# Decode attention over two caches: VectorE on whole key tiles, one normalization per side, another mapping of an output weight, and a projection split into three runs

## The chip, the cores and the metric

The kernel runs on one core of a Trainium2 chip. The engines of that core are TensorE (PE in the profile, its weight loads PEld), VectorE (DVE), ScalarE (ACT), GpSimd (POOL) and SyncE (SP), which issues most of the transfers; sixteen DMA engines carry them. The metric is the device time of one execution in microseconds (us), as the median of several runs. The profile is of one further execution, and its times are counted from the start of that execution's span.

## What is computed

Two independent attention layers, A and B, each decode one token. Both have 32 heads of 128 elements, an input row of 512, and a cache of 16384 positions for each head. A attends to all 16384 positions, B only to the last 4096. The two output rows of 512 stand side by side in the result. Everything is bf16.

```python
def _A_ref(x, k_cache, v_cache, wq, wo):
    B, Sq, D = x.shape
    Hq, Dh = 32, 128
    ...
    q = (lambda x, *d: x.transpose(*d))((x @ wq).reshape(B, Sq, Hq, Dh), 0, 2, 1, 3)
    ...
    scores = jnp.einsum("bhqd,bhkd->bhqk", q, k) * (Dh ** -0.5)
    p = _softmax(scores, axis=-1)
    o = jnp.einsum("bhqk,bhkd->bhqd", p, v)
    return (lambda x, *d: x.transpose(*d))(o, 0, 2, 1, 3).reshape(B, Sq, Hq * Dh) @ wo

# _B_ref: the same, with W = min(4096, max(256, Sk // 4)) and
    k = jnp.repeat(k_cache[:, :, Sk - W:, :], rep, axis=1)
    v = jnp.repeat(v_cache[:, :, Sk - W:, :], rep, axis=1)
```

All keys and values that are attended to are read once: 128 MB each of K and V for A, 32 MB each for B (in units of 2^20 bytes), and four weight matrices of 4 MB. The profile counts 352.32 million bytes read.

## The kernel before

**Tiles and steps.** The work runs in 20 steps (`steps`, `NT`), 16 of A and 4 of B; B's are steps 0, 7, 13 and 19. A step handles one key tile and one value tile of 128 partitions x 256 positions x 128 elements, 8.4 million bytes each. For A such a tile is two whole heads, with 64 partitions a head and 256 neighbouring positions a partition. For B it is two halves (`parts` is 2), each of four heads with 128 positions a partition, and each half is a transfer of its own (`b_window`).

**Buffers.** Key tiles live in a ring of two buffers (`kring`), value tiles in a single one (`vring`). At the start `wqt`, which holds both query weights, has the value buffer, and `scratch`, which holds the input rows `x_row` and B's spread input `xb`, has a key buffer. At the end the output weights and the last value halves take these buffers over (`wot`): `W` holds A's wo and the first half of B's last values, `Z` the second half and B's wo.

**Queries.** `spread_x` writes the input, turned into columns by `turn_x`, into a matrix with zeros elsewhere, so that one matmul leaves each partition the query of its own head. `project_q` makes the queries from it and ScalarE stores them in `s.q`.

**Scores on VectorE.** For each half of the tile `scores_prod` (L227) multiplies the keys in place by the query, and `scores_tree` folds the 128 elements to 64, 32, 16 and 8 by additions in place (L233), and to one by a reduction (L237) into `sc`.

**Softmax and the product with V.** A step does this for the tile of the step before (`un`): `unit_max` takes each partition's maximum (L244) and PE transposes it into one row; `max_all` takes the maximum of each head in that row (L262), copies it out to all partitions' places in `Mr` (L264, L266), and PE turns it back into a column (L268). `soft` makes the bias and the exponentials with their sums `cs` on ScalarE (L276, L282). `spread_p` writes the probabilities, masked by head, to `pm` (L297). `soft_sum` adds the sums of each head's partitions on PE (L315), `recip` takes the reciprocal on VectorE (L323), `pv` multiplies by the values on PE (L331), `evict` copies the result out, scaled by the reciprocal (L340), and `columns` picks each head's column and stores it in `s.O` (L348, L352). The last tile has a way of its own: `pv_columns` multiplies with the value half as the stationary operand (L358) and scales by the reciprocal as it stores (L362).

**Output.** `permute_o` reorders the 128 x 32 matrix of outputs by means of a shifted identity, `pick`, so that it fits the order of the rows in `wo_t`. Before, partition p holds the 32 neighbouring rows 32p to 32p + 31 of wo. `project_out_rows` (A) does 32 matmuls that add up one row (L383). `project_out_columns` (B) does 128 small matmuls that take wo as the stationary operand, piece by piece as wo arrives (L397), adds up the pieces (L403), turns the columns to rows (L407), and stores them (L409, L410).

**Order.** Within `tc.manual_schedule()` each engine runs its instructions in the order of the program text. SyncE issues the transfers in that order, too, and a transfer whose buffer is still in use holds up those after it. At the start the order is B's wq, the first half of B's first keys, A's wq, the second half, then the keys of step 1. The input rows come in three transfers each on ScalarE's queue. In step T the order is: the values of step T - 1 (`load_v`, L132 and L141), the keys of step T + 1 (`load_k`, L117 and L123), then on VectorE the first product, `max_all` of the tile before, the first tree, the reciprocal, the second product and tree, and `unit_max`. In step 19 A's wo and the first value half follow, and after the loop the second value half and B's wo in five pieces of 16, 8, 4, 3 and 1 rows a partition (L157).

## Time and profile before

| | |
|---|---|
| median of 3 runs | 825.79 us (825.49 to 826.01) |
| the profiled execution | 825.66 us |
| its span, first to last instruction | 823.9 us |
| mean granted TensorE clock in it | 0.592 |
| transferred | 352.62 MB, mean 428 GB/s |
| longest VectorE groups | additions L233 344.9 us in 160; products L227 277.8 us in 32 (A) and 69.4 us in 8 (B); reductions L237 48.8 us in 40 |
| product with V, L331 | 92.3 us in 1024 matmuls (A), 17.2 us in 192 (B) |

A page of the profile gives first the busy time of each engine with its share of the span and its number of instructions, and then the busy shares in tenths over 40 equal slices. The part on DMA queues names q1, the queue of the kernel's transfers, and others, among them q8 and q14, on which the engines fetch their instructions. The chain is followed back from the last instruction: at each step to what released it. In lists of instructions a line gives the start and the duration in us, the engine (SPq is SyncE's queue of DMA issues), the source line, the operation with output and input, how many instructions were merged, and in brackets how long the engine had been idle before and what ended that. In tables by windows the columns are the window, its length, the busy time of PE, PEld, VectorE, ScalarE and GpSimd, the granted TensorE clock, the busy share of the DMA engines and the rate in GB/s; a transfer packet is counted where it begins, so that single windows come out above 1.

### The profile page before, as it was taken

To read this page: it belongs to the slowest core of one execution; us is meant where nothing else is said; L and a number is where in the kernel's file an instruction comes from. 1 tells how busy PE (TensorE), PEld (TensorE's weight loads), DVE (VectorE), ACT (ScalarE), POOL (GpSimd) and SP (SyncE) were. 2 spreads that over 40 slices of the span, in tenths; PEclk is the share of its full clock that TensorE was granted. 3 is DMA by queue.
4 is the path that set the end of the run, shared out by engine and by line. 5 is a ranking of instruction groups with operands and counts; after the bars stand their busy time and mean duration, and the time that the engine had idled before them with its cause. 6 is when DMAs were issued, how large, how long until landed. Compare 5 with 4: busy or idle time off the path is not lost.

```text
span 823.9 us, 4724 instructions
## 1 busy us (share of the span) xinstructions
PE 202.7 (25%) x1985; PEld 100.7 (12%) x1985; DVE 763.9 (93%) x353; ACT 60.1 (7%) x168; POOL 0.7 (0%) x6
## 2 busy tenths in 40 slices
PE   2702212203030303130312213030303020303175
PEld 0201100101010101010101101010101010101035
DVE  2899999999999999999999999999999999999980
ACT  0101000001010000100000000010100000000010
POOL 0000000000000000000000000000000000000000
PEclk9865656565565555565555565565656565556585
DMA  9999999999999999999999999999999999999997
GB/s 384 434 433 433 453 420 443 430 436 440 423 446 420 424 439 443 412 453 420 443 417 449 414 452 410 450 417 428 438 449 424 436 433 430 443 414 445 418 429 296
DMA packets 8107, 352.62 MB, mean 428 GB/s; under 512 B 915, under 2 KB 1046, under 8 KB 1302
## 3 DMA queue, kind: packets, MB, share of 16 engines
q1 hardware_dynamic: 8072, 352.33, 99.2%
q8 instruction: 15, 0.25, 0.1%
q14 instruction: 6, 0.05, 0.0%
q10 hardware_dynamic: 14, 0.00, 0.0%
HBM read 352.32 MB, written 0.00 MB: 428 GB/s over the span
## 4 chain that ended last, share of the span: by engine, by line
DMA 82%; PE 15%; DVE 1%; SPq 0%; issue 0%; ACTq 0%; ACT 0%; DVEq 0%
DMA vt<-in_A_v_cache_dram 65%; DMA vt<-in_B_v_cache_dram 13%; PE oA L331 11%; DMA wot<-in_B_wo_dram 4%; PE oB L331 2%; PE qp L203 2%; DMA scratch<-in_A_x_dram 2%; DVE kt L227 1%; SPq L141 0%; ACTq L419 0%; SPq L157 0%; PE out_cols L397 0%; ACT qB L207 0%; PE out_rows L407 0%; DVE rows L409 0%
## 5 line engine op out<-in xcount | busy, mean ns | idle before, releaser
L233 DVE TENSOR_TENSOR kt<-kt 128x8192 bf16<-128x8192 bf16 (+3 forms) x160 | 344.9, 2156 | 4.8
L227 DVE TENSOR_TENSOR kt<-kt,qA 128x16384 bf16<-128x16384 bf16 x32 | 277.8, 8683 | 11.0 <-DMA kt<-in_A_k_cache_dram 10.9
L331 PE MATMUL oA<-vt,pm 128*8 128x512 bf16 x1024 | 92.3, 538 | 132.1 <-DMA vt<-in_A_v_cache_dram 132.1
L227 DVE TENSOR_TENSOR kt<-kt,qB 128x16384 bf16<-128x16384 bf16 x8 | 69.4, 8680 | 6.3 <-ACT qB L207 6.3
L249 PE MATMUL sm<-identf,m 128*1 128x128 f32 x24 | 8.1, 370 | 227.3 <-DVE m L244 227.3
L331 PEld LDWEIGHTS <-pm 128*8 128x8 bf16 (+1 forms) x1216 | 37.3, 111 | 216.7 <-issue 196.3
L268 PE MATMUL sm<-one_f,Mr 1*128 1x1 f32 x48 | 12.9, 347 | 176.7 <-DVE Mr L264 147.1
L237 DVE TENSOR_REDUCE sc<-kt 128x128 f32<-128x1024 bf16 x40 | 48.8, 1220 | 2.7
L276 ACT ACTIVATE bias<-sm 128x1 f32<-128x1 f32 (+1 forms) x20 | 3.4, 172 | 420.8 <-PE sm L268 420.8
L268 PEld LDWEIGHTS sm<-one_f,Mr 1*128 1x128 f32 x48 | 11.2, 298 | 183.6 <-DVE Mr L264 152.2
L249 PEld LDWEIGHTS sm<-identf,m 128*1 128x1 f32 x24 | 1.7, 79 | 229.3 <-issue 216.2
L340 ACT ACTIVATE o<-oA,r 128x512 f32<-128x512 f32 x16 | 11.0, 688 | 220.5 <-PE oA L331 220.5
L331 PE MATMUL oB<-vt,pm 128*16 128x512 bf16 x192 | 17.2, 494 | 20.3 <-DMA vt<-in_B_v_cache_dram 16.2
L348 PE MATMUL oc<-selA,o 128*128 128x2 f32 x128 | 16.9, 254 | 12.7 <-ACT o L340 12.7
L348 PEld LDWEIGHTS oc<-selA,o 128*128 128x128 f32 x128 | 15.5, 191 | 20.8 <-ACT o L340 20.8
L297 ACT ACTIVATE pm<-p,maskA 128x256 bf16<-128x256 bf16 x32 | 14.5, 500 | 0.5
L315 PE MATMUL sm<-cs,rowsA 128*128 128x1 f32 x32 | 9.4, 362 | 14.3 <-ACT p L282 14.3
L282 ACT ACTIVATE p<-sc,bias 128x256 bf16<-128x256 f32 (+1 forms) x24 | 11.3, 470 | 0.6
L203 PE MATMUL qp<-wqt,xbA 128*128 128x512 bf16 x32 | 8.8, 444 | 6.0 <-DVE kt L227 6.0
L315 PEld LDWEIGHTS sm<-cs,rowsA 128*128 128x128 f32 x32 | 8.0, 310 | 15.7 <-ACT p L282 15.7
L203 PE MATMUL qp<-wqt,scratch 128*128 128x512 bf16 x32 | 9.9, 486 | 0.0
L362 DVE TENSOR_TENSOR OB<-ocol,r 128x4 bf16<-128x4 f32 x2 | 0.3, 161 | 10.2 <-PE ocol L358 10.2
(71 smaller groups left out, 108.1 us busy)
## 6 DMA issues: line engine op xcount, KB each, us to landing
kt<-in_B_k_cache_dram SPq DMA_DIRECT2D x8, 4096.0 KB, 29.1
vt<-in_B_v_cache_dram SPq DMA_DIRECT2D x6, 4096.0 KB, 23.3
wot<-in_B_v_cache_dram SPq DMA_DIRECT2D x2, 4096.0 KB, 22.6
wqt<-in_B_wq_dram SPq DMA_DIRECT2D x1, 4096.0 KB, 12.3
wqt<-in_A_wq_dram SPq DMA_DIRECT2D x1, 4096.0 KB
wot<-in_A_wo_dram SPq DMA_DIRECT2D x1, 4096.0 KB
wot<-in_B_wo_dram SPq DMA_DIRECT2D x1, 2048.0 KB
wot<-in_B_wo_dram SPq DMA_DIRECT2D x1, 1024.0 KB
```

The source lines that it names most:

```text
L203: nc.tensor.matmul(qp[:, :, :], lhsT=s.xb[:, j, c, :], rhs=wq[:, c, j, g : g + 4, :], start=(k == 0), stop=(k == n - 1),)
L227: nc.vector.tensor_tensor(out=k, in0=k, in1=s.q[:, j : j + 1, :].broadcast_to([P, CH, DH]), op=ALU.mult)
L233: nc.vector.tensor_tensor(out=k[:, :, 0:w], in0=k[:, :, 0:w], in1=k[:, :, w : 2 * w], op=ALU.add)
L237: nc.vector.tensor_reduce(out=units[T].sc[:, u * CH : (u + 1) * CH], in_=k[:, :, 0:8], axis=AX.X, op=ALU.add)
L249: nc.tensor.transpose(un.sm[0:1, v * P : (v + 1) * P], m[:, v : v + 1], identf[:, :])
L268: nc.tensor.matmul(un.sm[:, 256 + v : 257 + v], lhsT=Mr[:, v * P : (v + 1) * P], rhs=one_f[:, :], start=True, stop=True,)
L282: nc.scalar.activation(out=un.p[:, v * n : (v + 1) * n], in_=un.sc[:, v * n : (v + 1) * n], func=ACT.Exp, scale=inv, bias=bias[:, v : v + ...
L297: nc.scalar.activation(out=out, in_=in_, func=ACT.Copy, scale=mask)
L315: nc.tensor.matmul(un.sm[v * w : (v + 1) * w, 264:265], lhsT=s.rows[:, :, :, :].rearrange("p r a b -> p (r a b)"), rhs=un.cs[:, v : v + 1] ...
L331: nc.tensor.matmul(s.o[r0 : r0 + un.rows, :], lhsT=un.pm[:, l, :, :].rearrange("p a b -> p (a b)"), rhs=V[un.T][:, 4 * l : 4 * l + 4, :], ...
L340: nc.scalar.activation(out=un.osb[:, :], in_=un.s.o[:, :], func=ACT.Copy, scale=un.r[:, 0:1])
L348: nc.tensor.matmul(oc[:, 0:w], lhsT=un.osb[:, j * P : (j + 1) * P], rhs=sel[:, j, :], start=(j == 0), stop=(j == 3),)
```

## The change

- `scores_prod` and `scores_tree` handle the whole tile: one product, four additions and one reduction a step instead of two of each. For B the product reads the queries of both halves. `max_all` thus comes after the whole product.
- The reciprocal and the scaling for each tile go away. `soft_sum` leaves each head's sum in `s.sums`, `columns` leaves the output without scaling in `s.Ou`, and `normalize` divides once for each side: for A within the last tree, after its second addition, for B before the last products with V. The sums are made the same way in every tile, so `s.rows` goes and `csm` is made in every tile.
- Small copies and fills move from VectorE to ScalarE (`xT`, the spread of x, the copy in `max_all`, `ident`, the zeros in the accumulators, `pick`) and to GpSimd (other fills).
- At the start both halves of B's first keys are asked for ahead of A's wq, and the input rows come in two transfers each.
- wo is mapped otherwise: partition p holds the rows of block 32(p mod 4) + p div 4, and `pick` follows. B's wo comes in pieces of 16, 8 and 5 rows a partition, and the last three rows in four transfers of 32 partitions each, whose outermost dimension has the size 8.
- At the end A's projection is split into three runs of 9, 4 and 19 rows, with `unit_max` and `max_all` of the last tile between them, and its row is stored later. The last tile's probabilities are all spread on ScalarE.

```diff
-    def load_wo(s, W, pieces):
+    def load_wo(s, W, pieces, low=0):
         s.wo_t = W.rearrange("p a b -> p (a b)").rearrange("p (r f) -> p r f", r=HQ)
-        src = s.wo.rearrange("(p r) f -> p r f", r=HQ)
+        flat = s.wo_t.rearrange("p r f -> p (r f)")
+        src = s.wo.rearrange("(b m r) f -> m b (r f)", b=4, r=HQ)
...
         for n in pieces:
-            nc.sync.dma_start(out=s.wo_t[:, r : r + n, :], in_=src[:, r : r + n, :])
+            nc.sync.dma_start(out=flat[:, r * DN : (r + n) * DN], in_=src[:, :, r * DN : (r + n) * DN])
             r += n
+        if low:
+            for a in range(0, P // 4, 8):
+                nc.sync.dma_start(
+                    out=flat[4 * a : 4 * a + 32, r * DN : (r + low) * DN],
+                    in_=src[a : a + 8, :, r * DN : (r + low) * DN],
+                )
...
     def make_masks(s):
         nc.vector.tensor_reduce(out=s.mask[:, :], in_=by_head(s, identf[:, :]), axis=AX.X, op=ALU.add)
-        n = 8 * s.groups // s.nh
-        nc.vector.tensor_copy(
-            s.rows[:, :, :, :], s.mask[:, :].unsqueeze(1).unsqueeze(3).broadcast_to([P, n, s.nh, 4])
-        )
...
                 dst = dst.rearrange("p c (i h) -> p c i h", h=s.nh)[:, :, :, j]
-            nc.vector.tensor_copy(dst, s.xT[:, :].unsqueeze(2).broadcast_to([P, KC, P // s.nh]))
+            nc.scalar.copy(dst, s.xT[:, :].unsqueeze(2).broadcast_to([P, KC, P // s.nh]))
...
-    def scores_prod(T, u):
+    def scores_prod(T):
         s, g = steps[T]
-        k = K[T][:, u * CH : (u + 1) * CH, :]
-        j = g if s is A else 2 * g + u
-        nc.vector.tensor_tensor(out=k, in0=k, in1=s.q[:, j : j + 1, :].broadcast_to([P, CH, DH]), op=ALU.mult)
-
-    def scores_tree(T, u):
-        k = K[T][:, u * CH : (u + 1) * CH, :]
+        k = K[T][:, :, :].rearrange("p (v l) d -> p v l d", v=s.parts)
+        q = s.q[:, s.parts * g : s.parts * (g + 1), :].unsqueeze(2)
+        nc.vector.tensor_tensor(out=k, in0=k, in1=q.broadcast_to([P, s.parts, 2 * CH // s.parts, DH]), op=ALU.mult)
+
+    def scores_tree(T):
+        k = K[T]
...
             nc.vector.tensor_tensor(out=k[:, :, 0:w], in0=k[:, :, 0:w], in1=k[:, :, w : 2 * w], op=ALU.add)
+            if w == DH // 4 and T == NT - 1:
+                normalize(A, HQ)
             w //= 2
-        if u == 0:
-            units[T] = Unit(T)
-        nc.vector.tensor_reduce(
-            out=units[T].sc[:, u * CH : (u + 1) * CH], in_=k[:, :, 0:8], axis=AX.X, op=ALU.add
-        )
+        units[T] = Unit(T)
+        nc.vector.tensor_reduce(out=units[T].sc[:, :], in_=k[:, :, 0:8], axis=AX.X, op=ALU.add)
+
+    def normalize(s, n):
+        nc.vector.reciprocal(s.sums[:, :], s.sums[:, :])
+        nc.vector.tensor_tensor(out=s.O[:, 0:n], in0=s.Ou[:, 0:n], in1=s.sums[:, 0:n], op=ALU.mult)
...
         if s is A:
-            nc.vector.tensor_copy(wide, Mv.unsqueeze(2).broadcast_to([1, s.nh, P // s.nh]))
+            nc.scalar.copy(wide, Mv.unsqueeze(2).broadcast_to([1, s.nh, P // s.nh]))
         else:
-            nc.vector.tensor_copy(wide, Mv.unsqueeze(3).broadcast_to([1, n, s.nh, P // s.nh]))
+            nc.scalar.copy(wide, Mv.unsqueeze(3).broadcast_to([1, n, s.nh, P // s.nh]))
...
         un.pm = pm[:, 0 : 2 * CH * s.nh].rearrange("p (i h c) -> p i h c", h=s.nh, c=4)
-        if un.last:
-            un.csm = small.tile([P, 8], F32, tag="csm", name="csm")
-            for v in range(s.parts):
-                nc.scalar.activation(
-                    out=un.csm[:, v * s.nh : (v + 1) * s.nh], in_=s.mask[:, :], func=ACT.Copy,
-                    scale=un.cs[:, v : v + 1],
-                )
+        un.csm = small.tile([P, 8], F32, tag="csm", name="csm")
+        for v in range(s.parts):
+            nc.scalar.activation(
+                out=un.csm[:, v * s.nh : (v + 1) * s.nh], in_=s.mask[:, :], func=ACT.Copy,
+                scale=un.cs[:, v : v + 1],
+            )
...
     def soft_sum(un):
         s = un.s
-        if un.last:
-            w = s.parts * s.nh
-            nc.tensor.matmul(
-                un.sm[:, 264 : 264 + w], lhsT=ones_col[:, :].broadcast_to([P, P]), rhs=un.csm[:, 0:w],
-                start=True, stop=True,
-            )
-            return
-        w = 32 * s.groups
-        for v in range(s.parts):
-            nc.tensor.matmul(
-                un.sm[v * w : (v + 1) * w, 264:265], lhsT=s.rows[:, :, :, :].rearrange("p r a b -> p (r a b)"),
-                rhs=un.cs[:, v : v + 1], start=True, stop=True,
-            )
-
-    def recip(un):
-        un.r = small.tile([P, 8], F32, tag="r", name="r")
-        n = un.s.parts * un.s.nh if un.last else 1
-        nc.vector.reciprocal(un.r[:, 0:n], un.sm[:, 264 : 264 + n])
+        w = s.parts * s.nh
+        nc.tensor.matmul(
+            un.sm[:, 264 : 264 + w], lhsT=ones_col[:, :].broadcast_to([P, P]), rhs=un.csm[:, 0:w],
+            start=True, stop=True,
+        )
+        nc.scalar.copy(s.sums[:, un.col(0) : un.col(0) + w], un.sm[:, 264 : 264 + w])
...
             nc.tensor.matmul(
-                op[:, :], lhsT=pick[:, 4 - j : 4 - j + P], rhs=oTs[:, j * HQ : (j + 1) * HQ],
+                op[:, :], lhsT=pick[:, 12 - 4 * j : 12 - 4 * j + P], rhs=oTs[:, j * HQ : (j + 1) * HQ],
...
-    def project_out_rows(s):
-        ps = ps_s.tile([1, DN], F32, tag="sp", name="out_row")
-        for r in range(HQ):
+    def project_out_rows(s, r0, r1):
+        if r0 == 0:
+            s.row_ps = ps_s.tile([1, DN], F32, tag="sp", name="out_row")
+        for r in range(r0, r1):
             nc.tensor.matmul(
-                ps[:, :], lhsT=s.Op[:, r : r + 1], rhs=s.wo_t[:, r, :], start=(r == 0), stop=(r == HQ - 1)
-            )
+                s.row_ps[:, :], lhsT=s.Op[:, r : r + 1], rhs=s.wo_t[:, r, :],
+                start=(r == 0), stop=(r == HQ - 1),
+            )
+
+    def store_row(s):
         row = one.tile([1, DN], BF16, tag="o4", name="row")
-        nc.scalar.copy(row[:, :], ps[:, :])
+        nc.scalar.copy(row[:, :], s.row_ps[:, :])
...
-    wo_pieces = (16, 8, 4, 3, 1)
+    wo_pieces, wo_low = (16, 8, 5), 3
...
             s.x_row = scratch[0:1, :, :].rearrange("p a b -> p (a b)")[:, x0 : x0 + D]
-            for a, b in ((0, D // 4), (D // 4, D // 2), (D // 2, D)):
+            for a, b in ((0, D // 2), (D // 2, D)):
...
         load_wq(B, wqt[:, 0:CH, :])
-        load_k(0, 0)
+        load_k(0)
         load_wq(A, wqt[:, CH : 2 * CH, :])
-        load_k(0, 1)
         make_identity(nc, identf[:, :])
-        nc.vector.memset(one_f[:, :], 1.0)
-        nc.vector.memset(one_b[:, :], 1.0)
-        nc.vector.memset(ones_col[:, :], 1.0)
-        nc.vector.memset(A.o[:, :], 0.0)
-        nc.vector.memset(B.o[:, :], 0.0)
-        nc.vector.tensor_copy(ident[:, :], identf[:, :])
+        nc.gpsimd.memset(one_f[:, :], 1.0)
+        nc.gpsimd.memset(one_b[:, :], 1.0)
+        nc.gpsimd.memset(ones_col[:, :], 1.0)
+        nc.scalar.copy(ident[:, :], identf[:, :])
...
             make_masks(s)
-        nc.vector.memset(pick[:, :], 0.0)
-        nc.vector.tensor_copy(
-            pick[:, 4 : 4 + P].rearrange("h (m k) -> h m k", k=4)[:, :, 0], identf[0:HQ, 0:HQ]
+            nc.scalar.activation(
+                out=s.o[:, :].rearrange("p (c m) -> p c m", c=4),
+                in_=identf[:, :].unsqueeze(1).broadcast_to([P, 4, P]), func=ACT.Copy, scale=0.0,
+            )
+        nc.gpsimd.memset(pick[:, :], 0.0)
+        nc.scalar.copy(
+            pick[:, 12 : 12 + P].rearrange("h (a t) -> h a t", t=16)[:, :, 0:4],
+            identf[0:HQ, 0:HQ].rearrange("h (t a) -> h a t", t=4),
...
                 pv(un)
-            scores_tree(T, 0)
-            if T >= 1:
-                recip(un)
...
                 columns(un)
-            scores_prod(T, 1)
-            scores_tree(T, 1)
+            scores_tree(T)
...
         load_v_half(NT - 1, 1, Z[:, 0:CH, :])
-        load_wo(B, Z[:, CH : 2 * CH, :], wo_pieces)
+        load_wo(B, Z[:, CH : 2 * CH, :], wo_pieces, wo_low)
...
         permute_o(A)
-        project_out_rows(A)
+        project_out_rows(A, 0, 9)
         unit_max(un)
+        project_out_rows(A, 9, 13)
         max_all(un)
+        project_out_rows(A, 13, HQ)
         soft(un)
-        spread_p(un, 0, CH)
-        spread_p(un, CH, 2 * CH, nc.vector.tensor_scalar_mul)
+        spread_p(un)
         soft_sum(un)
-        recip(un)
+        store_row(A)
+        normalize(B, un.col(0))
...
         permute_o(B)
-        project_out_columns(B, wo_pieces)
+        project_out_columns(B, wo_pieces + (wo_low,))
```

More of the change, by code (lines that the diff above doesn't have):

```diff
@@ L71 @@
     ones_col = singles.tile([P, 1], F32, tag="ones_col")
-    pick = singles.tile([HQ, P + 4], BF16, tag="pick")
+    pick = singles.tile([HQ, P + 12], BF16, tag="pick")
     A, B = _Side(), _Side()
@@ L82 @@
         s.groups = 4 // s.parts
-        s.rows = singles.tile([P, 8 * s.groups // nh, nh, 4], F32, tag=f"rows{n}", name=f"rows{n}")
+        s.Ou = singles.tile([P, HQ], F32, tag=f"Ou{n}", name=f"Ou{n}")
+        s.sums = singles.tile([P, HQ], F32, tag=f"sums{n}", name=f"sums{n}")
         s.sel = singles.tile([P, s.parts, nh * 4], F32, tag=f"sel{n}", name=f"sel{n}")
@@ L179, in turn_x @@
             )
-        nc.vector.tensor_copy(s.xT[:, :], ps[:, :])
+        nc.scalar.copy(s.xT[:, :], ps[:, :])
     def spread_x(s, flat):
         s.xb = flat[:, 0 : s.nh * KC * P].rearrange("p (h c m) -> p h c m", h=s.nh, c=KC)
-        nc.vector.memset(s.xb, 0.0)
+        nc.gpsimd.memset(s.xb, 0.0)
         turn_x(s)
@@ L339, in evict @@
         un.osb = one.tile([P, 512], F32, tag="o4", name="o4")
-        nc.scalar.activation(out=un.osb[:, :], in_=un.s.o[:, :], func=ACT.Copy, scale=un.r[:, 0:1])
+        nc.scalar.copy(un.osb[:, :], un.s.o[:, :])
     def columns(un):
@@ L351, in columns @@
             )
-        nc.scalar.copy(s.O[:, un.col(0) : un.col(0) + w], oc[:, 0:w])
+        nc.scalar.copy(s.Ou[:, un.col(0) : un.col(0) + w], oc[:, 0:w])
     def pv_columns(un, v, V_t):
@@ L363, in pv_columns @@
             out=s.O[:, un.col(v) : un.col(v) + s.nh], in0=oc[:, :],
-            in1=un.r[:, v * s.nh : (v + 1) * s.nh], op=ALU.mult,
+            in1=s.sums[:, un.col(v) : un.col(v) + s.nh], op=ALU.mult,
         )
@@ L455 @@
                 load_v_half(T, 0, W[:, CH : 2 * CH, :])
-            scores_prod(T, 0)
+            scores_prod(T)
             if T >= 1:
```

## The prediction

> **What bounds the kernel now.** I read the page first (busy shares, queues, the chain), then the chain in order of time, one middle step of the timeline, the last stretch by windows of 1 us, and the VectorE groups by form.
>
> From the page: VectorE is busy for 93%, but the data queue (q1) keeps the sixteen DMA engines busy for 99.2% of the span, and the chain is 82% transfers.
>
> ```profile
> PE 202.7 (25%) x1985; PEld 100.7 (12%) x1985; DVE 763.9 (93%) x353; ACT 60.1 (7%) x168; POOL 0.7 (0%) x6
> ...
> DMA  9999999999999999999999999999999999999997
> ...
> q1 hardware_dynamic: 8072, 352.33, 99.2%
> q8 instruction: 15, 0.25, 0.1%
> ...
> DMA 82%; PE 15%; DVE 1%; SPq 0%; issue 0%; ACTq 0%; ACT 0%; DVEq 0%
> ```
>
> The chain alternates between a V transfer and the product with V. That looks like a loop of load and compute, but a V load of 8.4 MB cannot need 33 us at 434 GB/s (19.3 us): it stands in the queue behind the next K tile.
>
> ```profile
> 436.97 32.84 DMA vt<-in_A_v_cache_dram
> 469.81 0.04 issue
> 469.86 5.24 PE oA L331 x61
> 475.10 0.02 issue
> 475.11 33.43 DMA vt<-in_A_v_cache_dram
> ```
>
> The timeline of the same step gives the slack.
>
> ```profile
> 436.97 0.33 SPq L132 DMA_DIRECT2D vt<-in_A_v_cache_dram  x1
> ...
> 449.57 0.33 SPq L117 DMA_DIRECT2D kt<-in_A_k_cache_dram  x1
> ...
> 450.48 8.69 DVE L227 TENSOR_TENSOR kt<-kt,qA 128x16384 bf16<-128x16384 bf16 x1 [0.48 <-DMA kt<-in_A_k_cache_dram]
> ...
> 461.12 0.91 ACT L297 ACTIVATE pm<-p,maskA 128x256 bf16<-128x256 bf16 x2
> ...
> 469.86 5.21 PE L331 MATMUL oA<-vt,pm 128*8 128x512 bf16 x64 [8.13 <-DMA vt<-in_A_v_cache_dram]
> ```
>
> A K tile lands at 450.4 and releases VectorE, which had waited 0.48 us. The next K request goes out at 449.6, and its data is due only when V has landed at 469.8: 20 us early. The next V request goes out at 475.1, due when that K has landed at about 489: 14 us early. So neither engine holds the transfers up; a step is 16.8 MB, 38.6 us. VectorE needs 38.25 us of it (second product to second product, 430.84 to 469.57, less 0.48 idle). It is nearly co-critical, but it is not the bound. I also chained the trace's packet records by start, duration and size: no 1 us slice between the first 3 us and the last 4 has a busy share below 0.97. Only the two ends can give time back.
>
> The last transfers do drain unevenly:
>
> ```profile
> 815.00:816.00 1.00, 0.68 (x20) 0.67 (x20) 0.00 (x0) 0.19 (x1) 0.00 (x0) 0.50 0.97 382
> 816.00:817.00 1.00, 0.42 (x16) 0.34 (x14) 0.00 (x0) 0.00 (x0) 0.00 (x0) 0.50 0.90 356
> 817.00:818.00 1.00, 1.00 (x43) 1.00 (x41) 0.00 (x0) 0.00 (x0) 0.00 (x0) 0.50 0.65 258
> 818.00:819.00 1.00, 1.00 (x39) 0.94 (x36) 0.00 (x0) 0.00 (x0) 0.00 (x0) 0.50 0.51 190
> 819.00:820.00 1.00, 0.61 (x18) 0.50 (x16) 0.00 (x0) 0.00 (x0) 0.00 (x0) 0.50 0.32 116
> ```
>
> The last two columns are DMA share and GB/s. By the packet chains six engines finish within 0.5 us of each other, two about 1.3 us later, eight 2.6 to 3.4 us after the first. The cause is in the same records: the 15 instruction fetches of q8 (16 KB, 1.02 to 1.11 us, and 0.41 to 0.66 us more on the neighbouring packet, so some 1.5 us) come round on eight engines only, two each. The engine that carries the x rows and A's output row has none of these and is among the first six to finish.
>
> **The change, part by part.**
>
> *Whole tiles.* Rows by form: product 8.683 us for 16384 elements, additions 4.415, 2.292, 1.225, 0.691, reduction 1.220; 18.53 a half, 37.05 a step. A whole tile takes the next row up: additions 8.68, 4.42, 2.29, 1.23; product 8.683 + 2 x (8.683 - 4.415) = 17.22; reduction 2.29 (the additions double with 0.16 us fixed). Sum 36.13, 0.92 less. The copy in max_all (0.215) goes to ScalarE and the reciprocal (0.158) goes away: 36.95 a step instead of 38.25. Worth nothing, since 38.6 us of transfer covers either; 20 x 1.3 = 26 us becomes idle time. B's product repeats q over one dimension more, which no row shows: below, the same rate (qA 8683, qB 8680 ns); above, the reduction's 0.84 elements per ns, 39 us a product. I take the first, as it is nearer; the other would cost tens of us and lies outside the range.
>
> *The softmax chain later in the step.* It now starts after 17.2 us instead of 8.6. In the step shown, pm was ready at 462.0; now 8.6 us later, plus the ScalarE copy (a 1x512 cast takes 0.575, the 1x128 some 0.25) and one csm (0.28): about 471, after V at 469.8. The V request slips by 1.3 us of its 14: nothing. Queued behind it on PE are only evict's columns and the next transposes, which come 10 us later.
>
> *The start.* B's K tile is now whole before VectorE starts: third of four transfers of 4.2 MB, where A's wq stood, which landed when PE started at 32.64. VectorE starts there instead of 23.89, 8.75 us late, and ends step 0 at 69.3 instead of 61.3. K(2), asked for at 69 instead of 61.26, is due at V(0)'s landing, 81.0. A's projection moves to the fourth landing, 42.3, and ends at 51; V(0) is asked for then, due at K(1)'s landing, 61.7. Step 1: product to 86.6, maxima 0.41, copy 0.4, PE 0.6, bias 0.17, exponentials 0.8, csm 0.47, four spreads 1.85 gives 91.4; product with V 5.1 gives 96.5. V(1) is due when K(2) lands, 81.0 + 19.3 = 100.3; with 1 us from request to first packet (0.73 to about 1.7 at the start) 2.5 us are left. Later steps gain 1.6 us each. So nothing, but this is the thinnest cover of the change. Fewer x transfers (four instead of six) and the set-up moved to ScalarE and POOL end before the first wq has landed at 13.
>
> *wo.* Main pieces 16, 8 and 5 rows go over all engines as before; the last three over eight. Packet rows: 3072 bytes 122 ns, 4096 160, 1024 46, so 38 ns a KB and about 198 for 5 KB. An engine without last rows now ends on 8 x 198 instead of 8 x (160 + 122 + 46): 1.0 us earlier. One with them has 16 x 122 on top: 0.9 us later. If the eight are those without q8 fetches, the drain ends 1.0 us earlier; if they are the loaded ones, 0.9 later. I take the first, because the engine with the single-row transfers has no fetches, though that is one engine of eight. Fetches of other engines (six of 8 KB, 0.7 to 1 us each) may eat some. After the last landing PE did 16 matmuls in 0.58; now the five-row piece may come last, with 20 + 12 behind it: 1.16. Net -0.4, so that PE would be done at 820.4 instead of 820.84.
>
> The Trainium skill (DMA: Bandwidth & Descriptors, "Why a DMA increments its semaphore by 16 and not by 1") says that a transfer runs on the largest number up to 16 that divides the slowest dimension of both sides, on the lowest-numbered engines, and its rules for kernel authors advise against a small outer dimension. By the rule the last rows go to engines 0 to 7, 0 among them; no view here shows the other seven's numbers.
>
> *PE at the end.* VectorE starts step 19 when both halves of K have landed (742.53 + 19.4 = 761.9, 0.6 later than 761.35) and normalizes A after the second addition, at 793.0. A's row projection starts at 794.3 instead of 791.1; it waits for the transposes (799.3) and the maxima, so 19 of its 32 matmuls stand ahead of soft_sum from 801.3 on. They took 0.43 us each at clock 0.5 and 0.21 at 1.0. The clock drops after the idle time, and returns after a full busy stretch of 3.4 us: between 804.2 and 808.0. So the rows end between 806.8 and 808.7, the two column products (3.55 and 3.58) at 814.4 to 816.3 instead of 814.1, and out_cols, which starts 1.45 later and needs 128 x 0.029 + 0.57, is done between 820.1 and 822.0. The middle, 821.05, is later than the transfers allow, and sets the end: +0.2.
>
> The Trainium skill (TensorE: Matmul & The Clock Gate, Part 1) says that these stretches are free-running windows, out of step with the kernel. The lengths in the clock record, multiples of 3.41 us, agree; by it the end would vary by up to 1.9 us from run to run.
>
> **Sum.** Start 0, middle 0, end +0.2: 825.66 of the profiled run (span 823.9 and 1.76 around it) becomes 825.9; the median is 0.13 above that run, so 826.0.
>
> **Rivals.** (1) *The eight engines are the loaded ones.* For: only one engine is placed. Against: that one is free of fetches. The drain ends at 821.15 instead of 820.24, with 12 matmuls behind it: 821.6, or PE's 822.0 at most: +0.75 to +1.2, 826.7. (2) *Slower: the first V request comes after the queue has run dry.* If the softmax chain of step 1 takes more than 2.5 us beyond my 9.9 (from 86.6 to 96.5), all engines stop after K(2), and each us beyond costs one, since nothing downstream can catch up transfers. For: nine ScalarE instructions in a row, priced from rows in which they did not queue so. Against: the same kind took 3 us in the middle. With 2.5 to 3.5 us of gap, 829. (3) *Faster: the drain becomes level*, with VectorE's fewer instructions sparing fetches and the clock in time. All sixteen finish at their mean, 1.75 us earlier, 824.0. Against: the rows above leave at most 1.0.
>
> **How the numbers follow.** Forecast 0.62 (own range 824.9 to 827.0), rival 1 0.20, rival 2 0.12, rival 3 0.06. A change under 0.2% (1.65 us) cannot be told from none here. Faster is rival 3, 0.06; slower is rival 2 and the tail of rival 1, 0.16; same 0.78. The range, 824.5 to 827.8, takes in the forecast, rival 1 and the bounds at the end.
>
> **What would show it.** Right: q1 still near 99% of a span within 1.6 us of 823.9; VectorE near 740 us busy with some 1.6 us idle before each product, released by K; first product at 32.6; V(1) asked for near 96.5; DMA shares in the last 4 us steeper or, by rival 1, with a longer foot; rows of A in three runs and column products ending at 814 to 816. Wrong: an empty slice of DMA anywhere in the middle, a product with V that starts late by more than 14 us, a product over 17.5 us on VectorE, or an end set by a chain I have not named.

## The result and the profile after

The changed kernel takes 829.14 us (median of 6 runs, 827.54 to 829.67) where the kernel before, on the same chip, takes 825.81 (825.49 to 826.01). The ratio is 1.0037 [1.0024, 1.005]: slower by some 3.3 us, not unchanged. Its runs also lie further apart, 2.1 us instead of 0.5. The profiled execution took 829.59, with a span of 827.7.

The page of the changed kernel (engines, queues, the chain, two groups of VectorE):

```profile
PE 204.9 (25%) x1979; PEld 98.8 (12%) x1979; DVE 736.1 (89%) x173; ACT 74.4 (9%) x242; POOL 3.6 (0%) x12
...
q1 hardware_dynamic: 7944, 352.33, 98.8%
...
DVE 53%; DMA 43%; PE 3%; issue 1%; SPq 0%; DVEq 0%; ACT 0%
...
L231 DVE TENSOR_TENSOR kt<-kt,qA 128x32768 bf16<-128x32768 bf16 x16 | 275.6, 17222 | 22.4 <-DMA kt<-in_A_k_cache_dram 22.4
...
L231 DVE TENSOR_TENSOR kt<-kt,qB 128x32768 bf16<-128x32768 bf16 x4 | 68.9, 17225 | 36.4 <-DMA kt<-in_B_k_cache_dram 36.4
```

VectorE lost 28 us of work, and the products now wait for K. The chain names VectorE for 53%, but that is no new bound: it leads through the work on VectorE that frees a K tile, while the product itself waits for its own K in each of the last 15 steps (1.2 to 2.8 us). The queue q1 is still at 98.8% of the span. The middle works as before; the time was lost at the ends.

In what follows, the column products are the two products of `pv_columns` with the halves of the last values (tile ocol, 128 matmuls each), and out_cols is `project_out_columns`. The timeline of PE at the end of the changed kernel (start, duration, line, tiles, count, and in brackets the idle time before it with its releaser):

```profile
799.38 0.59 PE L256 MATMUL sm<-identf,m 128*1 128x128 f32 x2 [1.11 <-DVE m L251]
...
802.63 6.07 PE L378 MATMUL out_row<-wot,OpA 128*1 128x512 bf16 x19
808.63 0.39 PE L313 MATMUL sm<-csm,ones_col 128*128 128x8 f32 x2
808.88 4.14 PE L352 MATMUL ocol<-pm,wot 128*128 128x4 bf16 x159
815.04 2.73 PE L352 MATMUL ocol<-pm,wot 128*128 128x4 bf16 x97 [2.02 <-issue]
...
819.19 0.83 PE L395 MATMUL out_cols<-OpB,wot 128*128 128x1 bf16 x26 [0.27 <-ACT OpB L372]
821.78 2.86 PE L395 MATMUL out_cols<-OpB,wot 128*128 128x1 bf16 x102 [1.77 <-issue]
```

The same stretch before:

```profile
804.34 3.55 PE L358 MATMUL ocol<-pm,wot 128*128 128x4 bf16 x128 [0.78 <-ACT pm L297]
810.55 3.58 PE L358 MATMUL ocol<-pm,wot 128*128 128x4 bf16 x128 [2.66 <-DMA wot<-in_B_v_cache_dram]
...
815.59 0.68 PE L397 MATMUL out_cols<-OpB,wot 128*128 128x1 bf16 x20 [0.27 <-ACT OpB L378]
816.84 2.19 PE L397 MATMUL out_cols<-OpB,wot 128*128 128x1 bf16 x76 [0.58 <-issue]
```

The column products start at 808.88; before, they started at 804.34. The two products now follow each other without the 2.66 us wait for V's last half that separated them before. PE stops in the second of them and again in out_cols, 2.02 and 1.77 us, with "issue" as releaser: no semaphore that the profile shows holds it. The windows at the second stop show the transfers running out (the last two columns are DMA share and GB/s):

```profile
819.00:820.00 1.00, 0.81 (x26) 0.77 (x26) 0.00 (x0) 0.14 (x1) 0.00 (x0) 0.50 0.40 100
820.00:821.00 1.00, 0.02 (x1) 0.00 (x0) 0.00 (x0) 0.00 (x0) 0.00 (x0) 0.50 0.14 37
```

The last transfer of wo ends at 821.4 in the packet records, while out_cols ends at 824.64. In this execution PE sets the end.

What comes with the stops is in the packet records: three instruction fetches of q8 (16 KB, 1.0 to 1.2 us) start at 812.67, 819.13 and 822.83 of the span, the first two just before the two stops. The records don't name the engine; that the fetches are PE's is read from their place and their number (15 in the run, where 1979 matmuls and as many weight loads are 15.5 blocks of 256). From the first stop to the second PE does 97 products of ocol, 1 of oT, 4 of op and 26 of out_cols: 128, with a weight load each 256 instructions. That is one fetch, if an instruction has 64 bytes (16 KB / 256). At the pace of the column products such a block is used up in about 3.6 us.

### The profile page after: what moved, and what is told of

Its sections match the earlier page's. It is cut to its first block, busy times and chain, and to the rows that moved or that the text cites. A ratio compares the mean times of both kernels' runs of the same rounds, so it can differ in the third digit from the quotient of the medians.

```text
span 827.7 us, 4592 instructions
## 1 busy us (share of the span) xinstructions
PE 204.9 (25%) x1979; PEld 98.8 (12%) x1979; DVE 736.1 (89%) x173; ACT 74.4 (9%) x242; POOL 3.6 (0%) x12
## 3 DMA queue, kind: packets, MB, share of 16 engines
q1 hardware_dynamic: 7944, 352.33, 98.8%
## 4 chain that ended last, share of the span: by engine, by line
DVE 53%; DMA 43%; PE 3%; issue 1%; SPq 0%; DVEq 0%; ACT 0%
DVE kt L231 25%; DMA kt<-in_A_k_cache_dram 24%; DVE kt L237 24%; DMA kt<-in_B_k_cache_dram 18%; DVE sc L242 3%; PE out_row L378 1%; PE ocol L352 1%; PE out_cols L395 0%; DVE m L251 0%; DVE M L269 0%; SPq L124 0%; PE sm L275 0%; PE sm L256 0%; SPq L148 0%; PE out_rows L405 0%
## 5 line engine op out<-in xcount | busy, mean ns | idle before, releaser
L237 DVE TENSOR_TENSOR kt<-kt 128x16384 bf16<-128x16384 bf16 (+1 forms) x80 | 332.2, 4153 | 2.1
L231 DVE TENSOR_TENSOR kt<-kt,qA 128x32768 bf16<-128x32768 bf16 x16 | 275.6, 17222 | 22.4 <-DMA kt<-in_A_k_cache_dram 22.4
L231 DVE TENSOR_TENSOR kt<-kt,qB 128x32768 bf16<-128x32768 bf16 x4 | 68.9, 17225 | 36.4 <-DMA kt<-in_B_k_cache_dram 36.4
L242 DVE TENSOR_REDUCE sc<-kt 128x256 f32<-128x2048 bf16 x20 | 45.7, 2286 | 1.9
L271 ACT COPY Mr<-M 1x128 f32<-1x128 f32 x16 | 4.7, 296 | 438.8 <-DVE M L269 438.8
L334 ACT COPY o<-oA 128x512 f32<-128x512 f32 x16 | 9.4, 585 | 94.1 <-PE oA L325 94.1
L342 PEld LDWEIGHTS oc<-selA,o 128*128 128x128 f32 x128 | 15.5, 191 | 19.2 <-ACT o L334 19.2
L313 PE MATMUL sm<-csm,ones_col 128*128 128x2 f32 (+1 forms) x40 | 11.6, 359 | 24.2 <-ACT csm L297 24.2
L313 PEld LDWEIGHTS sm<-csm,ones_col 128*128 128x128 f32 x40 | 9.8, 305 | 26.3 <-ACT csm L297 25.8
L378 PE MATMUL out_row<-wot,OpA 128*1 128x512 bf16 x32 | 11.9, 545 | 0.3 <-ACT OpA L372 0.3
L273 ACT COPY Mr<-M 1x256 f32<-1x256 f32 x4 | 2.6, 650 | 97.2 <-DVE M L269 97.2
```

Source lines behind the costliest of these rows:

```text
L231: nc.vector.tensor_tensor(out=k, in0=k, in1=q.broadcast_to([P, s.parts, 2 * CH // s.parts, DH]), op=ALU.mult)
L237: nc.vector.tensor_tensor(out=k[:, :, 0:w], in0=k[:, :, 0:w], in1=k[:, :, w : 2 * w], op=ALU.add)
L242: nc.vector.tensor_reduce(out=units[T].sc[:, :], in_=k[:, :, 0:8], axis=AX.X, op=ALU.add)
L313: nc.tensor.matmul(un.sm[:, 264 : 264 + w], lhsT=ones_col[:, :].broadcast_to([P, P]), rhs=un.csm[:, 0:w], start=True, stop=True,)
L334: nc.scalar.copy(un.osb[:, :], un.s.o[:, :])
L342: nc.tensor.matmul(oc[:, 0:w], lhsT=un.osb[:, j * P : (j + 1) * P], rhs=sel[:, j, :], start=(j == 0), stop=(j == 3),)
```

## The experiments

The theories were: (1) PE's order at the end: A's rows ahead of soft_sum push the column products back until they run without a pause, and the code for them comes late; (2) the last wo rows over eight engines; (3) the first V request, which comes later than before and can leave the queue empty. Each has experiments of its own below (some of the later expectations set up theories of their own, by number or letter), on the changed kernel (a part undone) or on the kernel before (a part done alone). Times are medians, with the range of all runs; the kernel before had 825.75 to 825.85 beside them.

### PE's order at the end

**Without the rows.** In the changed kernel 31 of the 32 matmuls of A's output row are left out, so that row of the output isn't the reference's.

```
-        for r in range(r0, r1):
+        for r in range(r0, min(r1, 1)):
```

> The changed kernel with 31 of the 32 matmuls of A's output projection left out (A's output row is then not the reference's). Theory 1 (the end is set by PE: 19 of A's row matmuls stand ahead of soft_sum, so the column products start at 809 instead of 804 and then run without the pause in which PE's next instructions used to be fetched): the first column product starts near 806, when the probabilities are spread, the stretches without a releaser (2.0 and 1.8 us) shrink to under 1.5 us together, and the time falls by 2 to 3.5 us to 825.5 to 827. Theory 2 (the drain of the transfers: the last rows go over eight loaded engines, or their requests wait): no change beyond 0.5 us, 828.5 to 829.5. Theory 3 (the start that came 8.7 us late opened a gap in the transfers): no change, 828.5 to 829.5.

Measured: 827.99 (826.76 to 829.82), ratio 1.0026 [1.0017, 1.0036]. Only 1.15 us fell away, less than theory 1 alone asked for, and its range reaches above that of the changed kernel. Its two stops, 0.24 and 1.77 us, are together above the 1.5 us that theory 1 allowed. Its profile shows another reason: the column products start at 807.08 instead of 808.88, but the last K landed 1.8 us later (the product on VectorE starts at 763.75 instead of 761.97), after a V request at 98.30. So a second loss, at the start, showed itself here.

**The runs alone, on the kernel before.** A's rows in three runs and the row stored late, nothing else of the change:

```
-        project_out_rows(A)
+        project_out_rows(A, 0, 9)
         unit_max(un)
+        project_out_rows(A, 9, 13)
         max_all(un)
+        project_out_rows(A, 13, HQ)
...
         soft_sum(un)
+        store_row(A)
```

> The kernel before with one part of the change alone: A's projection in runs of 9, 4 and 19 rows with the transposes and the maxima between them, and its row stored after soft_sum. Theory 1: the column products start near 808 instead of 804.3, PE stops once or twice without a releaser for 1 to 2 us, and the time rises by 1.5 to 3.5 us to 827.3 to 829.3. Theories 2 and 3: as before, 825.6 to 826.0, for neither the wo transfers nor the start is touched.

Measured: 828.69 (828.54 to 828.9), ratio 1.0034 [1.0021, 1.0047]: almost the whole loss, from this part alone, with wo, the start and VectorE as before. PE's timeline of this kernel:

```profile
802.74 5.74 PE L384 MATMUL out_row<-wot,OpA 128*1 128x512 bf16 x19
...
814.61 2.92 PE L358 MATMUL ocol<-pm,wot 128*128 128x4 bf16 x104 [1.99 <-issue]
...
820.81 3.05 PE L401 MATMUL out_cols<-OpB,wot 128*128 128x1 bf16 x109 [1.21 <-issue]
```

The same 19 rows, the same two stops, again 128 products apart (104 + 1 + 4 + 19). A's rows could have run from 790.9 here; the order of the program holds 19 of them back until 802.74. In the kernel before, all 32 ran in the 9 us ahead of the transposes, in time that nobody needed.

**Do the stops belong to the code or to the data?** 48 tiny matmuls at the start of PE's program shift all that follows by 48 products and read nothing of the tail:

```
+        pad = ps_s.tile([1, 1], F32, tag="sp", name="pad")
+        for _ in range(48):
+            nc.tensor.matmul(pad[:, :], lhsT=one_b[:, :], rhs=one_b[:, :], start=True, stop=True)
```

> The changed kernel with 48 matmuls of one element (96 PE instructions) added on PE in the first 8 us, where it waits for x. Theory 1 with the instruction fetch as the cause of the two stops: the stop in the column products moves 48 matmuls forward, from after 159 of the 256 to after 111, and the one that stood after 26 of the 128 out_cols matmuls moves into the second column product, to about its 113th; the time stays between 827.5 and 829.7, for the same number of blocks has to be fetched. If the stops belong to the operations themselves (a buffer, a clock stretch, a transfer) they stay after 159 and 26. Theories 2 and 3: no change, 828.5 to 829.5.

Measured: 828.99 (828.95 to 829.57), ratio 1.0039 [1.0024, 1.0053], the same time as the changed kernel (the profiled execution, with one stop instead of two, has a span 1.4 us shorter than that of the changed kernel; the median doesn't show this). The stop moved:

```profile
809.61 6.25 PE L352 MATMUL ocol<-pm,wot 128*128 128x4 bf16 x239
817.63 0.59 PE L352 MATMUL ocol<-pm,wot 128*128 128x4 bf16 x17 [1.77 <-issue]
```

159 - 48 = 111, and one block of 128 later is 239. There PE stops now; at 111 it didn't, and the 128 products of out_cols run without a stop. A wait for data would have stayed at its product. The kernel without the rows shifts the program the other way, by 31 products:

```profile
812.24 1.81 PE L352 MATMUL ocol<-pm,wot 128*128 128x4 bf16 x62 [1.61 <-DMA wot<-in_B_v_cache_dram]
814.30 1.90 PE L352 MATMUL ocol<-pm,wot 128*128 128x4 bf16 x66 [0.24 <-issue]
...
821.04 2.13 PE L394 MATMUL out_cols<-OpB,wot 128*128 128x1 bf16 x71 [1.77 <-issue]
```

Its first stop comes after 128 + 62 = 190 products, which is 159 + 31, and the second 128 products later (66 + 1 + 4 + 57). So the stops lie on block boundaries of the program.

Which boundaries become stops can be read from the packet records. The fourteen profiles of this document hold 20 such stops in the column products and out_cols. Each of them ends 1.26 to 1.57 us after the recorded end of a 16 KB fetch; PE had come to these boundaries at most 1.10 us after that end, or before it. At the boundaries there without a stop PE came 1.44 us or more after it. At 111 above, for example, the fetch had ended at 807.13 and PE came at 812.55. So the stops wait for the fetch.

**Normalize earlier.** In the changed kernel the second addition of the last tree is cut in two and A normalized between the halves, so that 20, 4 and 8 rows stand round the maxima; the last spread is split between ScalarE and VectorE as before.

```
+            cut = w == DH // 4 and T == NT - 1
+            for a, b in ((0, CH), (CH, 2 * CH)) if cut else ((0, 2 * CH),):
+                nc.vector.tensor_tensor(
+                    out=k[:, a:b, 0:w], in0=k[:, a:b, 0:w], in1=k[:, a:b, w : 2 * w], op=ALU.add
+                )
+                if cut and a == 0:
+                    normalize(A, HQ)
...
-        project_out_rows(A, 0, 9)
+        project_out_rows(A, 0, 20)
...
-        spread_p(un)
+        spread_p(un, 0, CH)
+        spread_p(un, CH, 2 * CH, nc.vector.tensor_scalar_mul)
```

> The changed kernel with its end mended in three places: A is normalized in the middle of the second addition of the last tree (that addition is split in two), A's row projection goes in runs of 20, 4 and 8, and the last probabilities are spread by ScalarE and VectorE together, as before. Theory 1: A's rows start near 792, the column products near 804.5, at most one stop of some 1 to 2 us is left, and the time falls by 2 to 3 us to 826 to 827.2. What is then left over 825.8 is theory 3's gap at the start. Theory 2: 828.5 to 829.5.

Measured: 827.91 (826.87 to 828.45), ratio 1.0025 [1.0015, 1.0034]. The column products start at 806.66, wait for V's half again, and only one short stop of 0.66 us is left; yet the time stays 0.7 us above the range expected. VectorE's timeline holds one reason:

```profile
764.19 17.23 DVE L231 TENSOR_TENSOR kt<-kt,qB 128x32768 bf16<-128x32768 bf16 x1 [1.98 <-DMA kt<-in_B_k_cache_dram]
```

With the order of loads of before (below) the queue stays full and this product begins at 762.0. Here the last K is 2.2 us late, in a profile of the slowest of the ten runs. Of the transfers behind it V's half is 2.1 us late (the second column product starts at 812.67, against 810.55 in the kernel with halves and early normalization below), but wo's last rows only 0.5 (822.49 against 821.95). The end now waits for wo's last rows.

### The start

**VectorE's whole tile on the order of loads of before.** Only the loads of step 0 are put back; VectorE still takes the tile whole.

```
-        load_k(0)
+        load_k(0, 0)
         load_wq(A, wqt[:, CH : 2 * CH, :])
+        load_k(0, 1)
```

> The changed kernel with the transfers of the start in the order of before (A's wq between the two halves of B's first keys), VectorE still on whole tiles. VectorE can then start only when the fourth transfer has landed, near 42.4 instead of 32.5. Theory 3 (the first V request comes when the queue of transfers has run dry, and each us of gap costs one): the request for V(1) goes out near 107 instead of 97.6, K(2) has landed at 100.3, the DMA engines stop for some 7 to 8 us, and the time is 835 to 838. Theory 1 alone (only the end matters): 828.5 to 830, as the gap would be absorbed.

Measured: 835.91 (835.33 to 838.43), ratio 1.0128 [1.0111, 1.0144], as theory 3 expected. The whole tile now waits for the fourth transfer, and V(1) is asked for at 106.59. The windows of this kernel:

```profile
92.00:100.00 8.00, 1.27 (x6) 1.19 (x6) 8.00 (x3) 2.40 (x10) 0.00 (x0) 0.50 1.00 434
100.00:107.00 7.00, 5.54 (x66) 2.00 (x66) 6.97 (x2) 1.73 (x6) 0.00 (x0) 0.67 0.01 2
```

The queue is dry for nearly 7 us, and the time is 6.8 us above that of the changed kernel. That the two agree so closely is partly luck: the last product starts 8.8 us later than in the changed kernel, at 770.81, and PE then lost less at the end (19 rows in 4.26 us instead of 6.07, stops of 1.15 and 1.21 us). The first stretch also says when: the data already asked for ends at 100. In the changed kernel the request goes out at 97.61, 2.4 us ahead of that.

**Step 0 in halves.** The changed kernel with the loads of before and step 0 in two halves, the rest of the change as it is:

```
-            scores_prod(T)
+            if T == 0:
+                scores_half(0)
+                scores_half(1)
+                unit_max(units[0])
+                continue
+            scores_prod(T)
```

> The changed kernel with step 0 alone in halves, and the transfers of the start in the order of before, so that VectorE starts at 23.9 again; all other steps on whole tiles, the end as changed. Theory 3: the request for V(1) goes out near 89 instead of 97.6, no slice near 100 has a DMA share under 0.97, and the time falls by 0.5 to 1.8 us, to 827.3 to 828.6, with less scatter than the 2.1 us of the changed kernel. Theory 1 alone: 828.5 to 829.5, unchanged.

Measured: 827.42 (826.72 to 828.49), ratio 1.0021 [1.0012, 1.003]. V(1) is asked for at 89.15, and the last product starts at 762.00. The median fell by 1.7 us, but not all of this need be the gap: in its profile, of the slowest of the ten runs, one stop of 2.44 us is left in the column products and none in out_cols. The range, 1.8 us, is hardly narrower than the 2.1 of the changed kernel. The cleaner measure of the gap is the pair with the earlier normalization, below.

### wo's last rows

**The old pieces.** The changed kernel with 16, 8, 4, 3, 1 rows over all sixteen engines:

```
-    wo_pieces, wo_low = (16, 8, 5), 3
+    wo_pieces, wo_low = (16, 8, 4, 3, 1), 0
```

> The changed kernel with B's wo in the five pieces of before (16, 8, 4, 3, 1 rows, all over sixteen engines), under the new mapping. Theory 1: the transfers are done before PE is, so no change beyond 0.5 us: 828.5 to 829.7. Theory 2: the drain ends 1 us earlier and with it the kernel, 827.5 to 828.3, or more if it sets the whole loss: 825.8. Theory 3: no change.

Measured: 827.68 (826.75 to 829.2), ratio 1.0023 [1.0013, 1.0033]: 1.5 us less than the changed kernel, within theory 2's range, but the ranges of the two kernels overlap. In its profile PE still sets the end, with stops of 1.50 and 1.22 us, and A's rows end at 807.41, 1.3 us earlier than in the changed kernel. So this run doesn't show what wo's pieces are worth; the next two do.

**The new rows alone, on the kernel before.** The mapping of wo, pick and the last three rows over eight engines:

```
-        src = s.wo.rearrange("(p r) f -> p r f", r=HQ)
+        src = s.wo.rearrange("(b m r) f -> m b (r f)", b=4, r=HQ)
...
-    wo_pieces = (16, 8, 4, 3, 1)
+    wo_pieces, wo_low = (16, 8, 5), 3
```

> The kernel before with the new mapping of wo alone, B's wo in pieces of 16, 8 and 5 rows and the last three in four transfers over eight engines. If the eight engines are those without PE's fetches: the drain ends up to 1 us earlier and the time is 825.0 to 825.8. If they are the loaded ones, or the last requests go out late (they wait for earlier transfers): 826.2 to 827. Theories 1 and 3 say nothing here, and the 3.3 us of the change do not come back.

Measured: 827.22 (826.7 to 827.54), ratio 1.0017 [1.0007, 1.0026]: 1.4 to 1.5 us lost, somewhat more than rival 1 gave and 0.2 above the range expected.

**The same mapping over sixteen engines.** As the last one, with pieces of 16, 8, 5 and 3 rows that all use sixteen engines:

```
-    wo_pieces, wo_low = (16, 8, 5), 3
+    wo_pieces, wo_low = (16, 8, 5, 3), 0
```

> The kernel before with wo mapped as in the change, in pieces 16, 8, 5 and 3 rows that all go over all sixteen engines. Theory A and theory B both: no part of the loss, 825.4 to 826.4, since neither late requests nor eight engines are left. If the mapping itself (partition blocks) or the coarser pieces cost: 826.8 to 827.5.

Measured: 825.99 (825.91 to 826.19), ratio 1.0 [0.9992, 1.0009]: nothing lost. So neither the mapping nor the coarser pieces cost; the four transfers over eight engines, in place of one over sixteen, do. In the packet records the last transfer of wo ends at 821.29 over eight and at 820.00 over sixteen. The windows of the kernel over eight engines, and then of this one over sixteen:

```profile
818.00:820.00 2.00, 1.96 (x73) 1.97 (x74) 0.00 (x0) 0.00 (x0) 0.00 (x0) 0.50 0.52 131
```

```profile
818.00:820.00 2.00, 1.48 (x56) 1.40 (x54) 0.00 (x0) 0.00 (x0) 0.00 (x0) 0.50 0.45 174
```

The share is higher over eight engines and the throughput lower. The packets are longer, too: the 128 of 5 KB take 30.1 us in sum instead of 25.5, the 128 of 3 KB 18.9 instead of 15.9. Two transfers that take turns on engines that are already late would explain this, but no view shows the single engines.

**The eight first.** Do they cost because of the engines, or because their four requests go out one after the other and late (on SP's queue they last 17.95 us in the kernel over eight engines, 24.50 in the changed kernel)? Here they are asked for ahead of the five-row piece, with the same bytes for each engine:

```
-    wo_pieces, wo_low = (16, 8, 5), 3
+    wo_pieces, wo_low = (16, 8, 3, 5), 2
...
+            if k == low:
+                for a in range(0, P // 4, 8):
+                    nc.sync.dma_start(out=flat[4 * a : 4 * a + 32, cols], in_=src[a : a + 8, :, cols])
```

> The kernel before with wo mapped as in the change, the three rows for eight engines asked for ahead of the five-row piece instead of behind it. Each engine has the same bytes as in the change, but the last request of wo no longer waits for a late transfer. Theory A (the last rows cost because their four requests go out late, one after the other, behind the landing of V's half and of A's row): most of the 1.4 us is gone, 825.4 to 826.3. Theory B (they cost because the eight engines that carry them are those with the instruction fetches, or because halves of 16 rows by eight packets are uneven): the drain keeps its long foot, 826.8 to 827.6.

Measured: 828.75 (828.1 to 828.98), ratio 1.0032 [1.002, 1.0043]: worse still, on theory B's side and beyond its range. The last request of wo goes out at 806.27, and the end comes later all the same. This doesn't quite rule theory A out: 806.27 is only 1.7 us before the four requests were through in the kernel with the new rows alone (807.92), and what goes out late is now the larger piece. The windows of this kernel:

```profile
816.00:818.00 2.00, 0.62 (x23) 0.53 (x21) 0.00 (x0) 0.00 (x0) 0.00 (x0) 0.50 0.89 219
```

A share of 0.89 at 219 GB/s is half of what sixteen engines move (434 at a share of 1.00, above), as if many packets shared few engines. The Trainium skill (DMA: Bandwidth & Descriptors, "Why a DMA increments its semaphore by 16 and not by 1") says that a transfer runs on the largest number of engines, up to 16, that divides the slowest dimension of both sides, and on the lowest-numbered ones, here eight; half the throughput agrees, though no view numbers the engines. Why the order made it worse by another 1.5 us, when each engine's bytes are the same, isn't settled: the sixteen-engine piece may have been held up behind the eight, and no run here tells this from another cause.

### All three undone

**Halves and early normalization.** The changed kernel with both of those edits, wo as in the change:

> The changed kernel with step 0 in halves on the order of loads of before, and A's normalization in the middle of the last tree's second addition (so that A's rows stand 20, 4, 8 round the maxima); wo as in the change. Theory 1 (three contributors: PE's chain at the end, the late first V request, the last wo rows over eight engines): two of the three are gone, and what is left is the wo part alone, which cost before 1.4 us: 826.4 to 827.5, with V(1) requested near 89, the 19th product near 762.0, column products done by 815 to 816, and an end that waits for transfers. Theory 2 (the gap at the start is not a cause, the two single repairs fell by chance): no further fall below the two single repairs, 827.4 to 828.2. Theory 3 (PE alone): all of the loss is gone, 825.4 to 826.2.

Measured: 826.88 (826.65 to 827.46), ratio 1.0012 [1.0003, 1.0021], as theory 1 expected. Beside the kernel with the early normalization alone (827.91) this is 1.0 us less, for the start alone (the ranges overlap, but by 0.6 us only); V(1) is asked for at 89.60, the last product starts at 762.05. What is left ends with two waits of PE for wo, 1.36 and 0.78 us.

**And wo over sixteen engines**, in the old pieces:

> The same with wo's pieces as before, 16, 8, 4, 3, 1 over all sixteen engines; left of the change are VectorE's whole tiles in steps 1 to 19, one normalization a side, set-up on ScalarE and POOL, and the fewer instructions. Theory 1: all three contributors are gone: 825.2 to 826.3, the time before. Theory 2: the part of the loss that none of the three explains stays: 826.8 or more. A fall below 825 would say that the change holds a gain hidden by the three.

Measured: 825.94 (825.76 to 826.7), ratio 1.0 [0.9992, 1.0009]: the time before. PE's timeline of this kernel:

```profile
804.53 3.45 PE L368 MATMUL ocol<-pm,wot 128*128 128x4 bf16 x128 [0.58 <-ACT sumsB L333]
810.72 3.57 PE L368 MATMUL ocol<-pm,wot 128*128 128x4 bf16 x128 [2.73 <-DMA wot<-in_B_v_cache_dram]
...
817.09 2.04 PE L411 MATMUL out_cols<-OpB,wot 128*128 128x1 bf16 x70 [0.54 <-issue]
```

The pause of 2.73 us for V's half is back, no stop in the column products, and 0.54 us of the one in out_cols. All of the loss is in the three parts; and what is left of the change, whole tiles above all, brings nothing either. No version here beats the kernel before.

## Why the prediction failed

**What held.** VectorE: a whole product takes 17.22 us as worked out, B's like A's; VectorE is busy for 736 us (forecast near 740) and waits for K before each of the last 15 products, and that gain is hidden by the transfers. The middle: in the step shown before, PE starts on V at 470.78 (forecast about 471), and the next V request slips from 475.1 to 476.64, 1.5 us of its 14 (forecast 1.3).

**The failed step: PE at the end.** It was forecast to be done between 820.1 and 822.0; it was done at 824.64. The order was read rightly, and the times up to the column products nearly hold: A's rows start at 794.28, the transposes at 799.38, the 19 rows start 1.3 us later than the 801.3 worked out and end at 808.70, at the late end of the range (806.8 to 808.7). The clock's part was read rightly, too: in the six profiles with this order the 19 rows take 4.26 to 6.42 us, a spread of 2.2 us beside the 1.9 of the forecast.

Then "the two column products (3.55 and 3.58)" were to end by 816.3 and ended at 817.77, and out_cols was priced at 128 x 0.029 + 0.57 and took 5.45 (819.19 to 824.64), 1.17 more. The sum had no stop in the column products, and the 0.57 was the one "issue" pause of the kernel before, taken as a constant. Each of these pauses is the uncovered rest of a fetch for code. Before, the fetch for the boundary in the second product ended at 809.12 and PE came there at 811.38, behind the wait of 2.66 us for V's half; without that wait it would have come at about 808.7 (an estimate, 811.38 - 2.66), before the fetch had ended. The change moved the products back by 4.5 us, that wait was gone, and PE came at 813.02, before its fetch had ended (813.76): the stop of 2.02 us. The moved work was counted; the cover that went with the wait was not.

The second stop, 1.77 us instead of 0.58, has another cause. No wait was lost ahead of it: PE needs some 5 us for that block in both kernels. But its fetch began 4.1 us after PE had entered the block, instead of 2.9 before. Why it began later isn't shown. The three runs alone, on the kernel before, cost 2.9 us, with both stops in their profile.

**wo.** The prediction took the eight engines to be those without code fetches and the drain 1.0 us shorter, from one engine of eight that could be placed. The part alone cost 1.4 us, as rival 1 had it (some 0.9), and the last transfer of wo ended at 821.29 (the rival's 821.15). The packets also got longer, which bytes alone don't tell. That the eight engines are the ones with the fetches, the rival's reason, isn't shown, for no view numbers them. It wasn't foreseen either that the four requests would wait on SP, for V's half and for A's output row. In the profiled execution PE was later still and hid this cost.

**The start.** "So nothing, but this is the thinnest cover of the change": 2.5 us were left by the forecast. V(1) was asked for at 97.61, 1.1 us later than the 96.5 worked out, because the product with V took 5.95 us instead of 5.1. The chain ahead of it came as forecast, 91.61 against 91.4. In the profiled execution nearly no time was lost (one slice of 1 us with a DMA share of 0.95, from the packet records). In other kernels with the same start the last product begins 0.5, 1.8 and 2.2 us later than in this one, with requests at 97.9 to 98.3 (in the one with the old pieces, asked for at 96.94, 0.1 us later). The request alone doesn't order them: 98.28 and 98.30 came with 0.5 and 1.8. Where PE no longer set the end the start cost 1.0 us. So rival 2 acted too, at a part of its price. The mean share of the DMA engines is only 0.2 to 0.3 us short round 100 in these three profiles; how that becomes 1.0 us at the end isn't shown. The start is also a part of the scatter: with PE repaired alone the range is 1.6 us wide, with halves in step 0 as well 0.8.

The three losses don't add: one at a time they come to 2.9 (PE), 1.4 (wo) and 1.0 (start), together to 3.3, since PE and the transfers end side by side and only the later one counts. The 0.62 for the forecast rested on treating them as rivals of which one at most comes true; each was a cost at another place, and they could all act in the same run.

## What to carry to other kernels

A wait that costs nothing can cover something else: before an order is changed so that engine work runs without a pause, ask what arrives during the pause (here 256 instructions of PE, used up in 3.6 us when each product is 0.03 us). Work that has a free place, as A's rows had before the transposes, shouldn't be moved to a place where others wait behind it. In a drain, read GB/s beside the share: a transfer over half of the engines keeps the share up while the throughput halves.

## What the runs showed of the hardware

- Stops at block boundaries of the program: 256 instructions of PE, 16 KB, fetches of 0.9 to 1.4 us in the record at the end of the fourteen profiles. The 20 stops last 0.24 to 2.44 us and end 1.26 to 1.57 us after the fetch in the record; PE was not stopped where it came 1.44 us or more after it. Between the two column products a wait of 2.0 to 2.8 us covered the fetch for the next boundary in all six profiles that have one, a wait of 1.2 to 1.6 us in none of three. The Trainium skill (Runtime: NRT & Kernel Launch, "Instruction fetch mechanics") has the blocks of 16 KB and 256 instructions, and calls the crossing "mostly hidden"; the shifted stops agree with the blocks, and where small matmuls use up a block in 3.6 us the crossing is not hidden.
- Four requests for eight engines, behind three for sixteen, held SP's queue for 18 to 24.5 us, while the three took 1.9. In the changed kernel they waited for A's output row and for V's half, which are other transfers. The eight engines need not be the reason: asked for last, the five-row piece over sixteen engines waited for A's output row, too (4.7 us). The profile doesn't say why.
